# Attention on one Trainium2 core: the last 64 queries of two steps scored in the four quarters of the TensorE array, zero rows under the last keys' values, and an attention order written out as a list

## The chip, the cores and the metric

One core of one Trainium2 chip. The metric is the time of one execution in microseconds of device time; the median of three is given. One further execution was profiled, and all rows below are from it. Engines: PE (TensorE; PEld are its weight loads), DVE (VectorE), ACT (ScalarE), POOL (GpSimd), SP (the queue that issues most DMAs). Each runs its own instructions strictly in the order of the program.

## What is computed

Causal attention in f32 for 2 batches of 12 heads, 448 tokens and head size 64, then two feed-forward layers of 896 tokens, 768 to 2048 to 768.

```python
scores = scale * np.matmul(q, k.transpose(0, 1, 3, 2))      # 2, 12, 448, 448
scores = np.where(mask, -1000000000.0, scores)              # keys after the query
attn = np.exp(scores - np.max(scores, axis=-1, keepdims=True))
attn = attn / (np.sum(attn, axis=-1, keepdims=True) + 1e-09)
x = np.matmul(attn, v)            # then heads side by side: 896 x 768
h = x @ w_in;  x = (h * np.clip(h + 3.0, 0.0, 6.0) / 6.0) @ w_out
h = x @ w2_in; x = (np.maximum(h, 0.0) + alpha * np.minimum(h, 0.0)) @ w2_out
```

## The kernel before

**Attention** goes in 12 steps (`Step`, 2 batches by 6 pairs of heads). The two heads of a pair are two sides: side 0 has rows 0 to 63 of the q and k tiles and side 1 rows 64 to 127, so that the scores of both sides can use two row halves of the array. The 448 queries are three chunks of 128 (chunks 0, 1, 2, with 128, 256 and 384 keys) and a tail of 64 queries with all 448 keys (chunk 3). The tail of both sides stands in one PSUM bank, side 0 on partitions 0 to 63 and side 1 on 64 to 127; with 64 rows and 64 columns each, its two matmuls use two opposite quarters of the array (L123). Per step:

- `scores` (L133 for chunks, L123 for the tail): PE writes q times k into banks of the pool `ps_s` (5 banks).
- `soften`: for each of 7 row groups DVE adds the mask and takes the maximum (L143), then ACT takes the exponential with its sum (L147).
- `normalise`: DVE takes the reciprocals (L151, L152), POOL multiplies the rows by them (L158); for the last step ACT does three of the rows (L156).
- `flip` 0 to 3: PE transposes four 128 by 128 blocks (L173) into a bank of `ps_t` (2 banks), DVE or ACT copies them out (L174). Flip 3 is the tail's.
- `weigh`: PE multiplies with v (L187 for chunks, L194 for the tail) into one bank of `ps_v` (1 bank); the fourth block of tail keys is keys 320 to 447, of which only the upper 64 rows are used (`keys = slice(D, P)`), a quarter of the array for each side.
- `gather`: ACT and DVE split the result into a high and a low part (L75, L76).

Every f32 matmul is two PE instructions. The order is a fixed software pipeline under a manual schedule: step n scores, step n-1 is normalised, step n-2 flipped, step n-3 weighed, step n-4 gathered. From n = 2 on each step also has one bite of `Pieces.convert`, five bites for each of the first three weight pieces, which ACT and DVE turn from 64-bit words into a high and a low part (L230 to L244). After the loop the last steps are flipped and weighed, and the first two units (`unit`, 18 matmuls each, in six bites) of the first layer go in between, in spare banks (tile name s).

**Feed-forward layers**: per unit or output tile three matmuls of 128 by 448 for each 128 rows (L266 to L268, f32r), while ACT and DVE convert the next weight piece and apply the activation. The first matmul whose output is named m begins that stage for good.

SP issues the loads of q, k and v for a step (L93 to L95) up to three steps ahead, and the raw weight pieces (L214).

Of the kernel before, what the change touches and what calls it, by code (L numbers as in the profile page):

```python
# [25 lines left out]
CUTS = ((0, 5), (5, 10), (10, 16))  # L26
ENGINES = {getattr(mybir.EngineType, n) for n in ("PE", "DVE", "Activation", "Pool", "SP")}
AHEAD = 5
MASK = -1.0e9 * D ** 0.5
SCALE = 1.0 / D ** 0.5  # L30


def f32(t):
# [3 lines left out]
class Step:  # L37


    def __init__(self, b, c):  # L40
        self.b, self.c = b, c


@with_exitstack
def fused_kernel(ctx: ExitStack, tc: tile.TileContext, q, k, v, w1i, w1o, w2i, w2o, alpha, out):
# [40 lines left out]

    def load(s):
        s.q = att.tile([P, S], F32, tag="q", name="q", bufs=4)  # L90
        s.k = att.tile([P, S], F32, tag="k", name="k", bufs=4)
        s.v = att.tile([P, 2, NCH + 1, D], F32, tag="v", name="v", bufs=6)
        nc.sync.dma_start(out=s.q, in_=q[s.c, :, s.b])  # L93
        nc.sync.dma_start(out=s.k, in_=k[s.c, :, s.b])
        nc.sync.dma_start(out=s.v, in_=v[s.c, s.b])  # L95

    def half(side):
# [5 lines left out]
    def begin(s):  # L103
        s.e = [att.tile([P, 6 * P], F32, tag="e", name="e", bufs=6) for _ in range(2)]
        s.et = att.tile([P, S], F32, tag="et", name="et")
        s.nm = att.tile([P, 7], F32, tag="nm", name="nm")
        s.sm = att.tile([P, 7], F32, tag="sm", name="sm")
        s.s, s.a = {}, {}

        s.rows = {}  # L110
        for j in range(NCH):
            for side in range(2):
                n = (j + 1) * P
                s.rows[j, side] = (s.e[side][:, OFF[j]:OFF[j] + n], mask[:, TAIL - n:TAIL], 2 * j + side)
        s.rows[NCH, 0] = (s.et, mask_tail, 2 * NCH)

    def scores(s, *chunks):

        if NCH in chunks:
            bank = ps_s.tile([P, BANK], F32, tag="s", name="s")[:, 0:S]  # L120
# [17 lines left out]
    def soften(s, *chunks):  # L138
        for j in chunks:
            for side in range(1 if j == NCH else 2):  # L140
                e, m, i = s.rows[j, side]
                nm, sm = s.nm[:, i:i + 1], s.sm[:, i:i + 1]
                nc.vector.tensor_tensor_reduce(  # L143
                    out=e, in0=s.s[j, side], in1=m, scale=-SCALE, scalar=3.0e38,
                    op0=ALU.add, op1=ALU.min, accum_out=nm,
                )
                nc.scalar.activation(e, e, AF.Exp, bias=nm, scale=-1.0, accum_out=sm)  # L147

    def normalise(s, others=()):
# [3 lines left out]
        for j, side in ((0, 0), (2, 0), (0, 1), (2, 1), (1, 0), (1, 1), (3, 0)):  # L153
            e, m, i = s.rows[j, side]
            if (j, side) in others:
                nc.scalar.activation(e, e, AF.Copy, scale=r[:, i:i + 1])  # L156
            else:
                nc.gpsimd.tensor_scalar(e, e, r[:, i:i + 1], 1.0, ALU.mult, ALU.mult)  # L158

    def flip(s, g, engine):  # L160


        t = ps_t.tile([P, BANK], F32, tag="t", name="t")
        if g < 2:
            todo = [(g, j, 0) for j in range(NCH)] + [(g, 2, 2)]
        elif g == 2:
            todo = [(side, j, 1) for side in range(2) for j in (1, 2)]
# [6 lines left out]
        (nc.scalar.copy if engine else nc.vector.tensor_copy)(a, t)  # L174
        if g < 2:
            s.a[g, 0], s.a[g, 2] = a[:, 0:TAIL], a[:, TAIL:BANK]
        elif g == 2:
            s.a[0, 1], s.a[1, 1] = a[:, 0:2 * P], a[:, 2 * P:4 * P]
        else:
            s.a["tail"] = a  # L180

    def weigh(s, bank=None):

        s.o = ps_v.tile([P, NT], F32, tag="o", name="o") if bank is None else bank
        for kc in range(NCH):
            for side in range(2):
# [12 lines left out]

# [121 lines left out]

    def attention():

        steps = [Step(b, c) for b in range(B) for c in range(KIN)]
        last = len(steps)
        loaded = 0
        runs = []
        ahead = [pieces.convert(i) for i in range(3)]

        def bites(run, count):  # L330
            for _ in range(count):
                next(run)

        for n in range(last):
            while loaded < min(last, n + 3):
                load(steps[loaded])
                loaded += 1
            if n == 1:
                pieces.load_to(1)
                nc.sync.dma_start(out=alpha_sb, in_=alpha)  # L340
            if n == 4:
                pieces.load_to(3)
            now, before, turned, weighed = (steps[n - i] if n >= i else None for i in range(4))
            if n == 0:
                begin(now)
                scores(now, 0, 2)
            scores(now, 1)
            soften(now, 0)
            if before:
                normalise(before)  # L350
            soften(now, 2)
            if turned:
                flip(turned, 0, 0)
                flip(turned, 1, n % 2)
            scores(now, NCH)
            if n >= 4:
                gather(steps[n - 4])
            soften(now, 1)
            if n + 1 < last:
                begin(steps[n + 1])  # L360
                scores(steps[n + 1], 0, 2)
            soften(now, NCH)
            if turned:
                flip(turned, 2, 1)
                flip(turned, 3, 0)
            if weighed:
                weigh(weighed)
            if n >= 2:
                next(ahead[(n - 2) // 5])

        def spare():
            return ps_s.tile([P, BANK], F32, tag="s", name="s")[:, 0:NT]

        runs.append(unit(0, 0, 0, *pieces.parts[0], spare()))
        normalise(steps[last - 1], ((2, 1), (1, 1), (NCH, 0)))
        for g in range(4):
            flip(steps[last - 2], g, g % 2)
        gather(steps[last - 4])
        bites(runs[0], 2)
        weigh(steps[last - 3])  # L380
        gather(steps[last - 3])
        weigh(steps[last - 2], spare())
        gather(steps[last - 2])
        bites(ahead[2], 1)
        for g in range(4):
            flip(steps[last - 1], g, g % 2)
        bites(ahead[2], 1)
        runs.append(unit(0, 0, 1, *pieces.parts[1], spare()))
        bites(runs[0], 3)
        weigh(steps[last - 1])  # L390
        gather(steps[last - 1])
        bites(runs[0], 1)
        bites(ahead[2], 3)
        bites(runs[1], 6)

    with ExitStack() as att_ctx:
        gp["first"] = ctx.enter_context(tc.tile_pool(name="g_first", bufs=1))
# [59 lines left out]
```

## Time and profile before

| | us |
|---|---|
| median of three runs (lowest, highest) | 566.55 (566.23, 566.59) |
| profiled execution | 566.77 |
| its span, first to last instruction | 564.9 |
| PE, DVE, ACT, POOL busy in the span | 551.8, 324.3, 320.3, 41.0 |
| first main-stage matmul (name m) starts at | 100.49 |

Busy time of PE is from modelled ends: two matmuls whose rows overlap count once. The start of one group of PE instructions to the start of the next (its pitch) tells what the group costs when PE never waits.

### The profile page before, as it was taken

How to read it: one execution, taken by the hardware profiler on the slowest of the kernel's cores; microseconds unless marked ns; L12 is line 12 of the kernel's file. 1: busy time of each engine (PE TensorE's matmuls, PEld its weight loads, DVE VectorE, ACT ScalarE, POOL GpSimd, SP SyncE). 2: the span in 40 equal slices, each digit the busy share in tenths (PEclk: the TensorE clock that was granted, in tenths of full speed). 3: DMA queues.
4: the chain of work that ended last, by engine and by line, in shares of the span. 5: the costliest groups of instructions: out<-in, count | busy, mean ns of one | idle time of the engine just before them, and what ended most of it. 6: DMA issues, size and time to landing. Idle time of an engine off the chain costs nothing.

```text
span 564.9 us, 7892 instructions
## 1 busy us (share of the span) xinstructions
PE 551.8 (98%) x3024; PEld 484.3 (86%) x3024; DVE 324.3 (57%) x577; ACT 320.3 (57%) x591; POOL 41.0 (7%) x92
## 2 busy tenths in 40 slices
PE   6999989999999999999999999999999999999997
PEld 3566657989999999999999999999999999999996
DVE  4888862588866576554444547777766634333400
ACT  6977773477665555443444457777777634344210
POOL 3745440000000000000000000000000000000000
PEclk9999999999999999999999999999999999999999
DMA  8363300145422233334333333333232343443000
GB/s 295 139 224 108 131 2 1 56 143 198 163 102 53 98 102 115 128 103 116 106 136 118 113 111 113 112 113 111 94 103 57 106 153 120 125 136 118 17 32 34
DMA packets 16885, 62.25 MB, mean 110 GB/s; under 512 B 2000, under 2 KB 6608, under 8 KB 16848
## 3 DMA queue, kind: packets, MB, share of 16 engines
q1 hardware_dynamic: 15120, 59.00, 31.8%
q10 hardware_dynamic: 1728, 2.75, 1.3%
q8 instruction: 24, 0.39, 0.3%
q14 instruction: 13, 0.11, 0.1%
HBM read 58.99 MB, written 2.75 MB: 109 GB/s over the span
## 4 chain that ended last, share of the span: by engine, by line
PE 85%; ACT 8%; DVE 4%; issue 2%; DMA 0%; SPq 0%; ACTq 0%; DVEq 0%
PE m L268 27%; PE m L266 27%; PE m L267 27%; ACT e L147 4%; PE t L173 1%; DVE e L143 1%; DVE a L174 1%; PE s L133 1%; ACT et L147 1%; PE o L187 1%; ACT xh L75 1%; ACT a L174 1%; DVE wf L238 0%; DMA k<-k_t 0%; DVE raw L235 0%
## 5 line engine op out<-in xcount | busy, mean ns | idle before, releaser
L266 PE MATMUL m<-gh,hi 128*128 128x448 f32 x384 | 140.2, 365 | 0.0
L268 PE MATMUL m<-gh,lo 128*128 128x448 f32 x384 | 140.2, 365 | 0.0
L267 PE MATMUL m<-gl,hi 128*128 128x448 f32 x384 | 140.2, 365 | 0.0
L268 PE MATMUL m<-xh,lo 128*128 128x448 f32 x372 | 135.7, 366 | 0.3 <-DVE lo L244 0.3
L267 PE MATMUL m<-xl,hi 128*128 128x448 f32 x372 | 136.0, 365 | 0.0
L266 PE MATMUL m<-xh,hi 128*128 128x448 f32 x372 | 135.9, 365 | 0.0
L244 DVE TENSOR_TENSOR lo<-wf,hi 128x768 fp32r<-128x768 f32 (+1 forms) x68 | 61.8, 911 | 88.0 <-ACT hi L242 86.1
L242 ACT CAST hi<-wf 128x768 fp32r<-128x768 f32 (+1 forms) x68 | 54.0, 796 | 83.9 <-PE m L267 80.1
L235 DVE SCALAR_TENSOR_TENSOR raw<-wf,raw 128x768 uint32<-128x768 uint32 (+1 forms) x68 | 61.9, 912 | 60.9 <-ACT wf L230 58.8
L233 ACT ACTIVATE raw<-raw 128x768 uint32<-128x768 uint32 (+1 forms) x68 | 59.3, 872 | 41.4 <-DMA raw<-w1o 17.2
L268 PEld LDWEIGHTS m<-gh,lo 128*128 128x128 f32 x384 | 72.1, 188 | 5.7
L267 PEld LDWEIGHTS m<-gl,hi 128*128 128x128 f32 x384 | 72.1, 188 | 5.7
L266 PEld LDWEIGHTS m<-gh,hi 128*128 128x128 f32 x384 | 72.1, 188 | 5.7
L268 PEld LDWEIGHTS m<-xh,lo 128*128 128x128 f32 x372 | 69.9, 188 | 6.3 <-DVE lo L244 0.7
L266 PEld LDWEIGHTS m<-xh,hi 128*128 128x128 f32 x372 | 69.9, 188 | 5.7
L267 PEld LDWEIGHTS m<-xl,hi 128*128 128x128 f32 x372 | 69.9, 188 | 5.7
L230 ACT ACTIVATE wf<-raw 128x768 f32<-128x768 f32 (+1 forms) x68 | 57.9, 851 | 22.1 <-DVE lo L244 22.1
L238 DVE SCALAR_TENSOR_TENSOR wf<-wf,raw 128x768 uint32<-128x768 uint32 (+1 forms) x68 | 61.8, 909 | 1.5
L75 ACT CAST gh<-hg 128x448 fp32r<-128x448 f32 x64 | 36.0, 562 | 36.9 <-DVE hg L276 20.5
L76 DVE TENSOR_TENSOR gl<-hg,gh 128x448 fp32r<-128x448 f32 x64 | 39.9, 623 | 23.9 <-ACT gh L75 23.6
L147 ACT ACTIVATE e<-e,nm 128x128 f32<-128x128 f32 (+2 forms) x72 | 35.8, 500 | 17.7 <-DVE nm L143 17.3
L158 POOL TENSOR_SCALAR e<-e,r 128x128 f32<-128x128 f32 (+1 forms) x70 | 32.0, 482 | 40.8 <-DVE r L152 14.8
(60 smaller groups left out, 406.4 us busy)
## 6 DMA issues: line engine op xcount, KB each, us to landing
raw<-w1i SPq DMA_DIRECT2D x16, 768.0 KB, 4.4
raw<-w2i SPq DMA_DIRECT2D x16, 768.0 KB, 4.4
raw<-w1o SPq DMA_DIRECT2D x12, 640.0 KB, 4.0
raw<-w2o SPq DMA_DIRECT2D x12, 640.0 KB, 4.1
raw<-w1o SPq DMA_DIRECT2D x6, 768.0 KB, 4.4
raw<-w2o SPq DMA_DIRECT2D x6, 768.0 KB, 4.4
v<-v_t SPq DMA_DIRECT2D x12, 256.0 KB, 3.6
q<-q_t SPq DMA_DIRECT2D x12, 224.0 KB, 4.3
```

The lines of the kernel that those rows point to most:

```text
L75: nc.scalar.copy(hi, src)
L76: nc.vector.tensor_sub(lo, src, f32(hi))
L147: nc.scalar.activation(e, e, AF.Exp, bias=nm, scale=-1.0, accum_out=sm)
L230: fixed(nc.scalar.activation(f32(w), f32(high), AF.Copy, scale=2.0 ** -112))
L233: fixed(nc.scalar.activation(low, low, AF.Copy, bias=-0.4999, scale=2.0 ** -29 * (1 - 2.0 ** -16)))
L235: fixed(nc.vector.scalar_tensor_tensor(out=low, in0=w, scalar=3, in1=low, op0=ALU.logical_shift_left, op1=ALU.bitwise_or))
L238: fixed(nc.vector.scalar_tensor_tensor(out=w, in0=w, scalar=0x80000000, in1=low, op0=ALU.bitwise_and, op1=ALU.bitwise_or))
L242: nc.scalar.copy(hi[:, 0:width], f32(w))
L244: nc.vector.tensor_sub(lo[:, 0:width], f32(w), f32(hi[:, 0:width]))
L266: nc.tensor.matmul(ps, lhsT=hi[:, w], rhs=xh, start=start, stop=False)
L267: nc.tensor.matmul(ps, lhsT=hi[:, w], rhs=xl, start=False, stop=False)
L268: nc.tensor.matmul(ps, lhsT=lo[:, w], rhs=xh, start=False, stop=stop)
```

## The change

`scores_tail` takes two steps: four matmuls of the tails, one for each quarter of the array. The second step of each pair is `odd`: its sides change places on the partitions of its bank (`at`). v gets 64 zero rows between key 384 and the last 64 keys, so that `weigh` uses all 128 rows for the fourth block too; the part of the last flip's output that belongs to the zero rows is there already. `attention` no longer has a loop over steps: it walks through the words of `PLAN`. The first letter is the function (s scores, t scores_tail of a pair, e soften, n normalise, f flip, w weigh, g gather, c a bite of convert, u a bite of a unit), two digits are the step (or the piece or unit), and the rest are its arguments: chunks; chunk and side; which of the seven rows ACT normalises; number and copying engine of the flip. Six matmuls on a zero tile stand in front. q and k have buffers for four steps, v for six; k of step 0 is issued from ACT's queue instead of SP's, v one step after q and k. The copies of the four flips have two buffers each, where all shared eight.

```diff
+QK_AHEAD, V_AHEAD = 4, 6
+WARM = 6
...
+PLAN = """
+s001 s0002 e0011 e0010 e0001 e0000 e0021 t00 s011 e0020 e0030 e0130 s0102 e0110 e0111 e0100 n00 e0101
+s021 e0121 s0202 e0120 e0211 e0210 e0200 e0221 e0201 e0220 t02 n0104 f000v f002v s0302 e0230 f003v f001v
+e0330 s031 e0311 e0300 n02 e0321 e0301 e0320 f011v f013v e0310 w00 t04 e0430 f010v f012v g00 s041 c00
+s0402 f023a e0421 e0420 n03 e0530 f021v e0401 e0411 e0410 w01 f020v f022v s051 g01 s0502 e0510 e0400
+e0521 e0511 f032v e0501 f031a e0520 w02 s061 n04 e0500 e0611 f033v g02 f030a s0602 t06 c01 e0610 n051
+e0621 f040v e0630 f042v e0600 e0620 e0601 w03 f041v f043v g03 s071 c01 s0702 e0720 f051a e0730 e0711 n06
+f053v w04 t08 e0710 e0701 e0700 e0721 e0830 f052v f050v n07 s081 g04 c00 s0802 e0810 e0811 e0801 f063v
+e0930 f060v w05 g05 f070a f062a s0902 e0800 e0820 e0821 f072v f061a e0901 s091 e0920 n080 e0900 e0910
+e0911 f071v f073a w06 e0921 s101 c01 g06 c01 s1002 f083a e1000 f081a n09 e1020 w07 e1011 e1021 e1001 t10
+f080a c01 e1010 e1030 f082v g07 s111 f091a f090a s1102 n102 f092a e1130 c00 f093a w08 c00 e1111 e1120
+e1121 e1110 f100v f101v e1101 w09s e1100 f103a c00 f102a n11234 u00 u01 c02 u01 f111v f112a g09 u01 g08
+c02 f110a f113v w10s w11 u00 u01 c02 u01 g11 u00 u00 g10 u00 c02 u00 c02 u01
+"""
...
-    def __init__(self, b, c):
-        self.b, self.c = b, c
+    def __init__(self, b, c, odd):
+        self.b, self.c, self.odd = b, c, odd
+        self.s, self.rows = {}, None
+
+    def at(self, side):
+        return side ^ self.odd
...
-        nc.sync.dma_start(out=s.k, in_=k[s.c, :, s.b])
+        queue.dma_start(out=s.k, in_=k[s.c, :, s.b])
+
+    def load_v(s):
+        s.v = att.tile([P, 2, NCH + 1, D], F32, tag="v", name="v", bufs=V_AHEAD)
...
-        if NCH in chunks:
-            bank = ps_s.tile([P, BANK], F32, tag="s", name="s")[:, 0:S]
-            for side in range(2):
-                d = half(side)
-                nc.tensor.matmul(bank[d], lhsT=s.q[d, TAIL:S], rhs=s.k[d, 0:S], start=True, stop=True)
-            s.s[NCH, 0] = bank
-            return
...
+    def scores_tail(*pair):
+
+        for s in pair:
+            s.s[NCH, 0] = ps_s.tile([P, BANK], F32, tag="s", name="s")[:, 0:S]
+        for s in pair:
+            for side in range(2):
+                d = half(side)
+                nc.tensor.matmul(
+                    s.s[NCH, 0][half(s.at(side))], lhsT=s.q[d, TAIL:S], rhs=s.k[d, 0:S], start=True, stop=True
+                )
...
-        a = att.tile([P, BANK], F32, tag="a", name="a", bufs=8)
+        a = att.tile([P, BANK], F32, tag=f"a{g}", name="a", bufs=2)
...
-            keys = slice(D, P) if kc == NCH else slice(0, P)
             for side in range(2):
                 nc.tensor.matmul(
-                    s.o[half(side), TAIL:S], lhsT=s.v[keys, side, kc],
-                    rhs=s.a["tail"][keys, kc * P + side * D:kc * P + (side + 1) * D],
+                    s.o[half(side), TAIL:S], lhsT=s.v[:, side, kc],
+                    rhs=s.a["tail"][:, kc * P:(kc + 1) * P][:, half(s.at(side))],
                     start=(kc == 0), stop=(kc == NCH),
                 )
...
+        warm = att.tile([P, P], F32, tag="warm", name="warm", bufs=1)
+        nc.vector.memset(warm, 0.0)
+        bank = ps_t.tile([P, BANK], F32, tag="t", name="t")
+        for _ in range(WARM):
+            nc.tensor.matmul(bank[:, 0:P], lhsT=warm, rhs=warm, start=True, stop=True)
+
+        for word in PLAN.split():
+
+            while qk < len(steps) and (qk < QK_AHEAD or scored[qk - QK_AHEAD] == 3):
+                load_qk(steps[qk], nc.sync if qk else nc.scalar)
+                qk += 1
+                while vs < min(len(steps), V_AHEAD + weighed, qk - 1):
+                    load_v(steps[vs])
+                    vs += 1
+                if qk == QK_AHEAD:
+                    pieces.load_to(1)
+                    nc.sync.dma_start(out=alpha_sb, in_=alpha)
+                elif qk == QK_AHEAD + 2:
+                    pieces.load_to(3)
...
+            what, n, rest = word[0], int(word[1:3]), word[3:]
+            s = steps[n]
+            if what == "s":
+                scores(s, *map(int, rest))
...
+            elif what == "t":
+                scores_tail(s, steps[n + 1])
...
+            elif what == "w":
+                weigh(s, spare() if rest else None)
...
-    vt = np.stack([vt[:, :, :, i:i + P] for i in (0, P, 2 * P, S - P)]).transpose(2, 1, 4, 3, 0, 5)
+    vt = np.insert(vt, [TAIL] * D, 0, axis=3).reshape(B, KIN, 2, NCH + 1, P, D).transpose(1, 0, 4, 2, 3, 5)
```

## Rows read from the trace of the kernel before

**Rows 1.** Busy time by stage: window, its length, then busy us (instructions) of PE, PEld, DVE, ACT, POOL, granted clock, DMA share and GB/s. The four windows are the start of attention, its steady steps, its end, and the feed-forward stage.

```profile
4.08:20.44 16.36, 14.71 (x84) 8.28 (x84) 12.41 (x60) 12.84 (x47) 7.73 (x17) 1.00 0.86 303
20.44:74.56 54.12, 54.11 (x481) 33.48 (x480) 44.23 (x161) 43.06 (x138) 27.13 (x57) 1.00 0.38 131
74.56:100.49 25.93, 22.48 (x193) 16.75 (x193) 11.28 (x24) 12.94 (x30) 3.95 (x9) 1.00 0.00 1
100.49:564.90 464.41, 460.50 (x2269) 425.70 (x2267) 256.35 (x335) 250.19 (x378) 0.00 (x0) 1.00 0.33 107
```

**Rows 2.** PE's timeline over one steady step: start us, us, line, operation, count. The last row is the same place in the next step.

```profile
27.15 0.97 PE L123 MATMUL s<-k,q 64*64 64x448 f32 x4
28.05 1.14 PE L133 MATMUL s<-k,q 64*128 64x128 f32 x8
29.12 0.66 PE L173 MATMUL t<-ident,e 128*128 128x128 f32 x4
29.61 0.60 PE L173 MATMUL t<-ident,et 128*128 128x128 f32 x4
30.14 1.52 PE L187 MATMUL o<-a,v 128*64 128x384 f32 x12
31.48 0.78 PE L194 MATMUL o<-a,v 128*64 128x64 f32 x16
32.19 0.70 PE L133 MATMUL s<-k,q 64*128 64x256 f32 x4
32.83 1.09 PE L173 MATMUL t<-ident,e 128*128 128x128 f32 x8
33.85 0.97 PE L123 MATMUL s<-k,q 64*64 64x448 f32 x4
```

**Rows 3.** PE's timeline, feed-forward matmuls: the first of the main stage and one 55 matmuls later.

```profile
100.49 0.37 PE L266 MATMUL m<-xh,hi 128*128 128x448 f32 x1
...
111.86 0.37 PE L267 MATMUL m<-xl,hi 128*128 128x448 f32 x1
```

**Rows 4.** PE's timeline in a window of 0.1 us around 20.5: the tail's instructions that run in it.

```profile
20.44 0.59 PE L123 MATMUL s<-k,q 64*64 64x448 f32 x2
```

**Rows 5.** PE's timeline in windows of 0.05 us: the end of one weigh, from its last two instructions on 128 rows (with the two behind them), from the first of the four on 64 rows, and the scores that follow.

```profile
25.07 0.43 PE L194 MATMUL o<-a,v 128*64 128x64 f32 x4
25.23 0.33 PE L194 MATMUL o<-a,v 64*64 64x64 f32 x4
25.49 0.49 PE L133 MATMUL s<-k,q 64*128 64x256 f32 x2
```

**Rows 6.** Timeline of all engines, the first 14 us (rows of the first step's way to its first flip).

```profile
0.73 1.28 ACT L147 ACT_TABLE_LOAD   x1 [0.73 <-PEq L447]
...
0.74 0.38 SPq L93 DMA_DIRECT2D q<-q_t  x1
...
1.17 0.42 SPq L94 DMA_DIRECT2D k<-k_t  x1
...
4.08 2.93 PE L133 MATMUL s<-k,q 64*128 64x128 f32 x12 [4.08 <-DMA k<-k_t]
...
6.28 0.29 DVE L143 CUSTOM_DVE_ANT_0 e<-s,mask 128x128 f32<-128x128 f32 x1 [6.28 <-PE s L133]
...
6.94 1.35 PE L123 MATMUL s<-k,q 64*64 64x448 f32 x4
...
10.95 2.75 POOL L158 TENSOR_SCALAR e<-e,r 128x128 f32<-128x128 f32 x6 [8.06 <-DVE r L152]
...
13.22 1.09 PE L173 MATMUL t<-ident,e 128*128 128x128 f32 x8
```

**Rows 7.** Busy time of L133 alone, in the first two microseconds of the first scores and in a steady step: the same eight instructions (chunks 0 and 2; where 10 stand, two are of the next group).

```profile
4.08:6.18 2.10, 2.10 (x10) 1.55 (x12) 1.00 0.88 206
28.05:29.12 1.07, 1.07 (x8) 0.52 (x8) 1.00 1.00 413
```

**Rows 8.** The page: clock granted to PE, in tenths of full speed over 40 equal slices, and the two copies of L174 that take the flips out (count, busy us, mean ns, idle us before them).

```profile
PEclk9999999999999999999999999999999999999999
...
L174 DVE COPY a<-t 128x512 f32<-128x512 f32 x29 | 19.4, 685 | 5.0 <-PE t L173 4.9
L174 ACT COPY a<-t 128x512 f32<-128x512 f32 x19 | 10.8, 567 | 1.9 <-PE t L173 1.9
```

**Rows 9.** Groups of instructions by line from 0 to 120 us: the rows that ACT normalises (count, busy us, mean ns, idle us before).

```profile
L156 ACT ACTIVATE e<-e,r 128x384 f32<-128x384 f32 (+1 forms) x2 | 1.0, 554 | 0.5 <-DVE r L152 0.5
```

**Rows 10.** Busy time by step, in the columns of rows 1: the first and the last of eight steps from one tail to the next.

```profile
20.44:27.15 6.71, 6.71 (x62) 4.15 (x61) 4.32 (x19) 6.71 (x23) 4.37 (x10) 1.00 0.04 13
...
67.44:74.56 7.12, 7.12 (x61) 4.43 (x60) 6.83 (x29) 6.07 (x20) 4.52 (x10) 1.00 0.32 112
```

**Rows 11.** What PE waited for from 8 to 110 us: us in total, times, longest.

```profile
PE t L173 <- ACT a L174: 2.4, 3, 1.1
PE t L173 <- DVE a L174: 1.2, 2, 0.9
PE o L187 <- DVE xl L76: 0.9, 2, 0.6
```

**Rows 12.** Timeline of SP and ACT: the load of the fourth raw weight piece, and the next L230 on ACT after those of the first three pieces.

```profile
59.63 0.37 SPq L214 DMA_DIRECT2D raw<-w1i  x1
...
109.89 0.91 ACT L230 ACTIVATE wf<-raw 128x768 f32<-128x768 f32 x1
```

More of the change, by code (lines that the diff above doesn't have):

```diff
@@ L84, in split_x, with load_qk @@
         xs[blk, c] = (xh, xl)
[L89 to L92, printed above, removed]
+    def load_qk(s, queue):
+        s.q = att.tile([P, S], F32, tag="q", name="q", bufs=QK_AHEAD)
+        s.k = att.tile([P, S], F32, tag="k", name="k", bufs=QK_AHEAD)
         nc.sync.dma_start(out=s.q, in_=q[s.c, :, s.b])
-        nc.sync.dma_start(out=s.k, in_=k[s.c, :, s.b])
+        queue.dma_start(out=s.k, in_=k[s.c, :, s.b])
+    def load_v(s):
+        s.v = att.tile([P, 2, NCH + 1, D], F32, tag="v", name="v", bufs=V_AHEAD)
         nc.sync.dma_start(out=s.v, in_=v[s.c, s.b])
@@ L107, in begin @@
         s.sm = att.tile([P, 7], F32, tag="sm", name="sm")
-        s.s, s.a = {}, {}
+        s.a = {}
         s.rows = {}
@@ L136, in scores, with soften, normalise @@
             at += n
[L138 to L145, printed above, removed]
-                )
-                nc.scalar.activation(e, e, AF.Exp, bias=nm, scale=-1.0, accum_out=sm)
-    def normalise(s, others=()):
+    def scores_tail(*pair):
[6 more added lines that the diff above has]
+                    s.s[NCH, 0][half(s.at(side))], lhsT=s.q[d, TAIL:S], rhs=s.k[d, 0:S], start=True, stop=True
+                )
+    def soften(s, j, side):
+        if s.rows is None:
+            begin(s)
+        e, m, i = s.rows[j, side]
+        nm, sm = s.nm[:, i:i + 1], s.sm[:, i:i + 1]
+        nc.vector.tensor_tensor_reduce(
+            out=e, in0=s.s[j, side], in1=m, scale=-SCALE, scalar=3.0e38,
+            op0=ALU.add, op1=ALU.min, accum_out=nm,
+        )
+        nc.scalar.activation(e, e, AF.Exp, bias=nm, scale=-1.0, accum_out=sm)
+    def normalise(s, others):
         r = att.tile([P, 7], F32, tag="r", name="r")
@@ L152, in normalise @@
         nc.vector.reciprocal(r, r)
-        for j, side in ((0, 0), (2, 0), (0, 1), (2, 1), (1, 0), (1, 1), (3, 0)):
-            e, m, i = s.rows[j, side]
-            if (j, side) in others:
+        for n, row in enumerate(((0, 0), (2, 0), (0, 1), (2, 1), (1, 0), (1, 1), (NCH, 0))):
+            e, m, i = s.rows[row]
+            if n in others:
                 nc.scalar.activation(e, e, AF.Copy, scale=r[:, i:i + 1])
@@ L173, in flip @@
             nc.tensor.transpose(t[:, i * P:(i + 1) * P], e, ident)
-        (nc.scalar.copy if engine else nc.vector.tensor_copy)(a, t)
+        (nc.scalar.copy if engine == "a" else nc.vector.tensor_copy)(a, t)
         if g < 2:
@@ L322, in attention @@
     def attention():
[L324 to L327, printed above, removed]
+        steps = [Step(b, c, c % 2) for b in range(B) for c in range(KIN)]
         ahead = [pieces.convert(i) for i in range(3)]
[L330 to L394, printed above, removed]
+        units = {}
+        scored, weighed, qk, vs = [0] * len(steps), 0, 0, 0
+        warm = att.tile([P, P], F32, tag="warm", name="warm", bufs=1)
+        nc.vector.memset(warm, 0.0)
@@ new lines, in attention @@
+        bank = ps_t.tile([P, BANK], F32, tag="t", name="t")
[13 more added lines that the diff above has]
+                    pieces.load_to(3)
+            while vs < min(len(steps), V_AHEAD + weighed, qk):
+                load_v(steps[vs])
+                vs += 1
+            what, n, rest = word[0], int(word[1:3]), word[3:]
+            s = steps[n]
+            if what == "s":
+                scores(s, *map(int, rest))
+                scored[n] += 1
+            elif what == "t":
+                scores_tail(s, steps[n + 1])
+                scored[n] += 1
+                scored[n + 1] += 1
+            elif what == "e":
+                soften(s, int(rest[0]), int(rest[1]))
+            elif what == "n":
+                normalise(s, tuple(map(int, rest)))
+            elif what == "f":
+                flip(s, int(rest[0]), rest[1])
+            elif what == "w":
+                weigh(s, spare() if rest else None)
+                weighed += 1
+            elif what == "g":
+                gather(s)
+            elif what == "c":
+                next(ahead[n])
+            elif what == "u":
+                if n not in units:
+                    units[n] = unit(0, 0, n, *pieces.parts[n], spare())
+                next(units[n])
@@ L396, in fused_kernel, with spare @@
+    def spare():
+        return ps_s.tile([P, BANK], F32, tag="s", name="s")[:, 0:NT]
     with ExitStack() as att_ctx:
```

## The prediction, made before the changed kernel ran

> **What bounds the kernel now.** I read the page first, then busy time by stage, PE's timeline over one step, the timeline of the start and the waits of PE. By stage [rows 1]: PE is busy 54.11 of 54.12 us in the steady steps, 460.50 of 464.41 in the feed-forward stage, but 14.71 of 16.36 at the start of attention and 22.48 of 25.93 at its end. DVE is busy 82% (44.23 of 54.12) and ACT 80% (43.06) in the steady steps and far less elsewhere. So the feed-forward stage is PE's from 100.49 us to the end, and a change of attention is worth what it moves the first main-stage matmul.
>
> PE's busy time hides overlap, so I count by pitch. A steady step [rows 2]: tail 0.90, chunks 0 and 2 1.07, flips 2 and 3 0.49 + 0.53, weigh 1.34 + 0.71, chunk 1 0.64, flips 0 and 1 1.02; together 6.70 (27.15 to 33.85), without a wait. The 36 matmuls of the two units that lie in attention cost 0.207 each ((111.86 - 100.49) / 55 [rows 3]), 7.44 in all. PE's work up to 100.49 is 12 x 6.70 + 7.44 = 87.84; the other 12.65 us are losses. I split them at the bounds of the stages [rows 1], with the pitches of the steady step [rows 2]:
> - **a**, before the first matmul: 4.08.
> - **b**, 4.08 to 20.44: 16.36 less the work done in it, which by the loop is four chunk pairs 0 and 2 (4.28), four chunks 1 (2.56), three tails (2.70) and six flips (3.06), 12.60: 3.76.
> - **c**, 20.44 to 74.56: 54.12 less 8 x 6.70: 0.52.
> - **d**, 74.56 to 100.49: 25.93 less the remaining 21.64: 4.29.
>
> **The change, part by part.**
>
> *Tails in four quarters.* Now a tail is four instructions of 448 columns in a pitch of 0.90; two of them run at the same time, both in flight from 20.44 on [rows 4], so each two cost 0.45. The change issues eight for two steps. If four run at once a pair of steps costs little over 0.90; if still only two, 4 x 0.45 = 1.80, as now. Between 0.90 and 1.80 I take 0.95: the rows that use column halves at once (weigh's two sides) and row halves at once (chunks' two sides) both show overlap, chunks 0 and 2 having 2 x (128 + 384) columns in 1.07 where the tail's 896 need 0.90 [rows 2], and the four quarters are the product of the two. The extra 0.05 is for four more instructions (16 small ones of weigh's tail cost 0.71, 0.044 each, partly hidden). Gain: 12 x 0.90 - 6 x 0.95 = 5.10.
>
> Two instructions at once in one PSUM bank is also where a rule of the Trainium skill can be held against the trace. Today's two quarters lie on different rows, write the same bank and start together [rows 4]. The Trainium skill's page TensorEngine Tiling (Array Packing), section Gotcha 1: PSUM Pressure, says that different row tiles can't reach the same PSUM bank at the same time. By that rule each bank's two matmuls would take turns, the best would be two at a time, and this part would gain nothing; the trace disagrees, since it shows two in one bank.
>
> *Zero rows under v.* The four instructions of the last block run on 64 rows; the first of them start 0.16 after the last two on 128 rows [rows 5], where two instructions at weigh's mean pitch take 0.09. The 0.07 over is what I give to the change of shape, 12 x 0.07 = 0.84; bounds 0 and 12 x 0.16 = 1.9. The multiplications by zero add no instructions; v's transfer keeps its size.
>
> PE's work thus falls by 5.94.
>
> *The start (a).* k of step 0 goes from the second place in SP's queue to ACT's. It was issued at 1.17 and used at 4.08, 2.91 later [rows 6]. Issued at 0.74 it is there at 3.65; issued after the 1.28 us table load that now begins at 0.73, it is there at 4.92. The table load belongs to the first exponential, which stands behind the load in the program, so I take the early side. The six zero matmuls lie on PE ahead of the scores: at the slow pace of the first scores (2.10 for 512 columns on each side [rows 7]) 128 columns cost 0.52, six 3.2; begun after a memset at about 1.0, they end near 4.2, so they can hold the scores by half a microsecond. I take 3.9 for a: -0.18.
>
> *The first rounds (b).* The first eight score instructions took 2.10 against 1.07 later [rows 7], and the first tails 1.35 against 0.97 [rows 6, 2], although the page shows the granted clock at full speed (2.4 GHz) throughout [rows 8]; before them PE was idle. DVE's first operation waited for all eight (6.28), and everything after it in the first rounds is the chain DVE, ACT, POOL up to the first flip at 13.22 [rows 6]. The plan scores chunk 1 first, four instructions, 0.64 at full or 1.26 at half pace, so DVE begins at about 4.6 to 5.2, 1.1 to 1.7 earlier; I take 1.4, and 0.4 for the tail at full pace. The first flip stands after 20 softens in the plan, yet needs only the normalised rows of step 0, so it comes earlier by the same amount. b = 3.76 - 1.8 = about 2.0: -1.76. Bounds 0.6 (no loss but the chain's own) and 3.76.
>
> *The steady order (c).* DVE and ACT keep their work: the plan has 29 flips copied by DVE and 19 by ACT, as now [rows 8], and the same softens, gathers and bites. Only eight rows are normalised on ACT instead of three, 5 x 0.55 = 2.8 at most [rows 9], of over 90 us. But PE's eight steps shrink from 53.6 to 49.6, so DVE rises from 82% to about 88%. The first of the eight steps has DVE busy 4.32 of 6.71 and ACT 6.71; the last has DVE 6.83 of 7.12 and is 0.42 longer than the rest [rows 10]: when DVE is near full, PE waits. Between 0.52 as now and 8 x 0.42 = 3.4 I take 1.5: +0.98. The fixed lists make this sensitive: a late e on DVE holds every flip copy and xl behind it, and by them PE's next transposes and weigh.
>
> *The end (d).* PE's waits are for copies a and for xl [rows 11]: the last two steps' flips stand next to each other, with two banks and nothing else to do. The plan puts w08, w09 and half-microsecond bites of units between them, and between g and the next w. I leave one wait of the size seen (0.9) and 0.8 for refilling: 1.7, -2.59; bounds 0.8 and 4.29.
>
> *What lies under cover.* Raw pieces 1 and 2 are queued on SP right behind k of step 5, 1.5 MB or 5 us at the 303 GB/s of the start [rows 1]; behind them wait v of step 5 and q of step 6, first used after w02, over 10 us later. Without that cover each would be up to 5 us late. v is issued one step after q and k, and is first read by w00, word 48 of the plan. Raw piece 3 waits for the third bite of piece 0, now just before w08, near 70 us instead of the issue at 59.63; ACT first reads it at 109.89 [rows 12], about 100 after the change, so some 25 us are spare. The feed-forward stage needs piece 2 one unit pair (36 matmuls, 7.4 us) after its start, and the plan ends its bites before that start. I count 0.
>
> **The sum.** -5.94 - 0.18 - 1.76 + 0.98 - 2.59 = -9.49. The profiled execution took 566.77 for a span of 564.9, so 1.87 lie outside; 555.41 + 1.87 = 557.28. It lay 0.22 above the median, so the median forecast is 557.1.
>
> **Rivals.**
> - *The written order brings nothing*: b, c and d stay as they are, because losses on PE reappear as waits for DVE and ACT at 88%. For it: the 7.12 step. Against: the waits at the end have an empty DVE and ACT (11.28 and 12.94 of 25.93 [rows 1]). Only the work and a count: -6.12, 560.4. With c at its bound of 3.4, 563.3.
> - *Only two quarters at a time*: the change then doesn't do what its name says. The tails keep 1.80 a pair, +5.10, 562.2. The bank rule of the Trainium skill named above would be one such cause. Against: both kinds of overlap are seen [rows 2].
> - *Slower: quarters take turns one by one.* Eight instructions at 0.45 cost 3.60 a pair, 2.65 over the forecast, +15.9: 573.0. Decisive from 0.95 + 9.49 / 6 = 2.53 a pair on. For it: nothing here shows two instructions sharing rows and two sharing columns at once. Against: today's two opposite quarters overlap [rows 4].
>
> **How the numbers follow.** Forecast 0.70, order brings nothing 0.20, two at a time 0.06, one by one 0.04. Predicted time 557.1. The forecast's own bounds: quarters at 0.90, full 1.9 for zero rows, a 3.65, b 0.6, c 0.52 and d 0.8 would be 5 lower, and not all at once; I take 553.2 as the low end. The upper end, 562.2, takes in the order that brings nothing and reaches the two at a time. A measurement of this kernel can tell about 0.2% (1.1 us) from no change. Only one by one is slower: 0.04; within 0.2% only where an order worse than bounded eats both gains: 0.02; faster 0.94.
>
> **What will show it.** The first main-stage matmul near 91 instead of 100.49. The pitch of a double tail near 0.95 in PE's timeline; 1.8 or more proves the second or third rival. Weigh's tail below 0.71. DVE's first operation before 5.3. Waits of PE in the end below 2 us, and some new waits for DVE or ACT in the middle. The feed-forward stage as long as before, 464.4. The prediction is wrong if the main stage starts after 96, or if it grows by a wait for converted pieces.

## The result and the profile after

| | before | after |
|---|---|---|
| median, us | 566.57 | 552.96 |
| ratio (95% interval) | | 0.9763 (0.9746 to 0.978) |
| span of the profiled execution | 564.9 | 550.9 |
| first main-stage matmul (name m) | 100.49 | 86.78 |
| feed-forward stage from there | 464.41 | 464.12 |

The kernel is 13.6 us faster. The forecast was 557.1 with a range from 553.2 to 562.2: the sign was right, the gain was too small by 4.1 us, and the time lies 0.24 below the range. Most of the 4.1 comes from one step of the prediction, the waits that it expected in the middle and at the end of attention (terms c and d). All of the gain but 0.3 us is attention's: the main stage begins 13.71 earlier. A few executions, of the kernel before too, are some 9 us longer; all medians here and below leave them out.

PE's timeline after the change (start, us, line, operation, count), first the first rounds, then a steady stretch, the two waits and the first main-stage matmul. These rows answer to the steady step [rows 2] and to the weigh's end [rows 5]; the last one is the same as [rows 3].

```profile
6.24 0.98 PE L168 MATMUL s<-k,q 64*64 64x448 f32 x8
7.15 2.99 PE L156 MATMUL s<-k,q 64*128 64x256 f32 x18
10.83 1.13 PE L156 MATMUL s<-k,q 64*128 64x128 f32 x6 [0.69 <-DVE nm L177]
11.89 0.98 PE L168 MATMUL s<-k,q 64*64 64x448 f32 x8
12.81 1.09 PE L207 MATMUL t<-ident,e 128*128 128x128 f32 x8
...
18.93 0.64 PE L227 MATMUL o<-a,v 128*64 128x64 f32 x16
19.50 0.98 PE L168 MATMUL s<-k,q 64*64 64x448 f32 x8
20.41 1.09 PE L207 MATMUL t<-ident,e 128*128 128x128 f32 x8
21.43 1.57 PE L156 MATMUL s<-k,q 64*128 64x256 f32 x12
22.93 0.66 PE L207 MATMUL t<-ident,et 128*128 128x128 f32 x4
...
23.96 1.52 PE L221 MATMUL o<-a,v 128*64 128x384 f32 x12
...
58.86 0.66 PE L207 MATMUL t<-ident,et 128*128 128x128 f32 x4 [0.89 <-POOL et L192]
...
70.11 1.00 PE L207 MATMUL t<-ident,e 128*128 128x128 f32 x7 [0.39 <-POOL e L192]
...
86.78 0.36 PE L299 MATMUL m<-xh,hi 128*128 128x448 f32 x1
```

A double tail costs 0.91 (19.50 to 20.41), where two tails cost 1.80. Weigh's tail costs 0.57 (18.93 to 19.50) instead of 0.71. Chunk 1 with chunks 0 and 2 right behind it costs 1.50 (21.43 to 22.93), where they cost 0.64 + 1.07 apart. And from 20 us to the main stage PE waits only twice for longer than 0.2, both times for POOL.

PE's timeline after, in a window of 0.04 us behind 19.52, answers to [rows 4]: four instructions in flight from 19.50 on.

```profile
19.50 0.61 PE L168 MATMUL s<-k,q 64*64 64x448 f32 x4
```

The start after, all engines [rows 6]: k of step 0 issued by ACT (its table load stands behind it, at 1.17), the zero matmuls, the first scores and DVE's first operation.

```profile
0.74 0.40 ACTq L121 DMA_DIRECT2D k<-k_t  x1
...
1.05 2.93 PE L367 MATMUL t<-warm 128*128 128x128 f32 x12 [1.05 <-DVE warm L364]
...
4.13 2.18 PE L156 MATMUL s<-k,q 64*128 64x256 f32 x12
...
5.52 0.42 DVE L177 CUSTOM_DVE_ANT_0 e<-s,mask 128x256 f32<-128x256 f32 x1 [4.52 <-PE s L156]
```

Busy time by stage after, in the columns of [rows 1]: start, middle, end, feed-forward stage.

```profile
4.13:19.50 15.37, 14.63 (x117) 9.30 (x117) 13.80 (x65) 13.51 (x51) 6.95 (x15) 1.00 1.02 391
19.50:69.39 49.89, 49.01 (x493) 33.14 (x489) 44.73 (x153) 45.32 (x140) 29.75 (x55) 1.00 0.33 104
69.39:86.78 17.39, 17.00 (x156) 14.14 (x153) 9.59 (x25) 11.65 (x28) 3.73 (x8) 1.00 0.27 91
86.78:550.90 464.12, 460.23 (x2269) 425.54 (x2267) 256.75 (x336) 249.73 (x379) 0.00 (x0) 1.00 0.32 105
```

DVE and ACT are busy 90% and 91% of the middle, more than the 88% of the prediction, and PE idles 0.9 of 49.9.

**The prediction's sum with measured terms.** Work after: 12 x (6.70 - 0.90 - 0.14) + 6 x 0.91, and 36 unit matmuls at 0.203: 80.70. The loss is the rest of 86.78, 6.08, split as before: 4.13 before the first scores; from there to 19.50, 15.37 less 13.65 of work; the middle to 69.39, 49.89 less 49.94; the end, 17.39 less 17.11. The work is counted with the old order's pitches for all groups but the tails, so a group that the new order makes cheaper shows as a smaller loss; that is why the middle comes out at -0.05.

| term | forecast | measured |
|---|---|---|
| tails in four quarters | -5.10 | -5.34 |
| zero rows | -0.84 | -1.68 |
| a, before the first scores | -0.18 | +0.05 |
| b, first rounds | -1.76 | -2.04 |
| c, middle | +0.98 | -0.57 |
| d, end | -2.59 | -4.01 |
| unit matmuls 0.203 instead of 0.207 | | -0.12 |
| sum | -9.49 | -13.71 |
| feed-forward stage | 0 | -0.29 |

### The profile page after: what moved, and what is told of

Its sections match the earlier page's. It is cut to its first block, busy times and chain, and to the rows that moved or that the text cites. A ratio compares the mean times of both kernels' runs of the same rounds, so it can differ in the third digit from the quotient of the medians.

```text
span 550.9 us, 7924 instructions
## 1 busy us (share of the span) xinstructions
PE 543.8 (99%) x3036; PEld 484.8 (88%) x3036; DVE 325.0 (59%) x578; ACT 321.5 (58%) x596; POOL 42.6 (8%) x87
## 4 chain that ended last, share of the span: by engine, by line
PE 94%; DVE 2%; POOL 1%; DMA 1%; ACT 1%; issue 1%; POOLq 0%; ACTq 0%
PE m L301 27%; PE m L299 27%; PE m L300 27%; PE t L207 4%; PE s L156 3%; PE o L221 2%; POOL e L192 1%; PE s L168 1%; PE o L227 1%; DVE e L177 1%; DMA k<-k_t 1%; PE s L221 1%; PE s L299 0%; PE s L301 0%; PE s L300 0%
## 5 line engine op out<-in xcount | busy, mean ns | idle before, releaser
L192 POOL TENSOR_SCALAR e<-e,r 128x128 f32<-128x128 f32 (+2 forms) x64 | 32.4, 526 | 32.5 <-DVE nm L177 15.2
```

## The experiments

Before was run beside all of them (medians 566.5 to 566.8). Differences below are of medians, against the 552.96 of the changed kernel unless another is named. The theory: PE sets the time of the new order, so each PE term counts in full, and the order removed most waits. The main rival: DVE and ACT, 90% busy, set it.

### Quarters, alone undone

```diff
-        steps = [Step(b, c, c % 2) for b in range(B) for c in range(KIN)]
+        steps = [Step(b, c, 0) for b in range(B) for c in range(KIN)]
```

> The changed kernel, but both steps of a pair of tails use the same two opposite quarters (no step is odd); order, zero rows and start stay. Theory (four quarters at once is worth its pitch): a double tail takes 4 x 0.45 = 1.80 instead of 0.91 on PE, 6 x 0.89 = 5.3 us more, 558.3. Rival (DVE and ACT, 90% busy in the middle of the changed kernel, pace it): part of the 5.3 lies in time in which PE would have waited, 2 us more or less, near 555.

Measured 556.51: 3.6 more; the profiled spans differ by 4.1 (555.0), the main stage begins at 90.98, 4.2 later. PE's timeline of this run, the second and the third double tail and the main stage:

```profile
12.38 1.72 PE L168 MATMUL s<-k,q 64*64 64x448 f32 x8
14.04 1.09 PE L207 MATMUL t<-ident,e 128*128 128x128 f32 x8
...
20.73 1.72 PE L168 MATMUL s<-k,q 64*64 64x448 f32 x8
...
90.98 0.36 PE L299 MATMUL m<-xh,hi 128*128 128x448 f32 x1
```

Two tails that take turns in the same quarters cost 1.66, not 1.80: two tails next to each other cost 0.14 less than two apart. Undoing the quarters thus adds 6 x 0.75 = 4.5 to PE's work, and most of it (3.6 to 4.2) reaches the end. The expected 5.3 took 1.80 for the pair. From the third double tail to the main stage it takes 70.25, after the change 67.28: the four double tails there (4 x 0.75 = 3.0) count in full, so PE does set the time of middle and end, and the rival's 2 us is out.

### Zero rows, alone undone

```diff
         for kc in range(NCH + 1):
+            keys = slice(D, P) if kc == NCH else slice(0, P)
...
-                    s.o[half(side), TAIL:S], lhsT=s.v[:, side, kc],
-                    rhs=s.a["tail"][:, kc * P:(kc + 1) * P][:, half(s.at(side))],
+                    s.o[half(side), TAIL:S], lhsT=s.v[keys, side, kc],
+                    rhs=s.a["tail"][keys, kc * P:(kc + 1) * P][:, half(s.at(side))],
```

> The changed kernel, but the fourth block of weigh's tail uses only the upper 64 rows again (the zero rows are loaded and not used). Theory (the change of shape costs PE, as the pitch of weigh's tail shows, 0.57 against 0.71): 12 x 0.14 = 1.7 us more, 554.6. Rival (the pitch difference comes from what stands behind it): no difference.

Measured 554.09 (three runs, 553.8 to 555.1), 1.1 more, two thirds of what was expected. PE's timeline of this run, one weigh's tail and the double tail behind it:

```profile
43.79 0.72 PE L228 MATMUL o<-a,v 128*64 128x64 f32 x14
...
45.26 1.09 PE L207 MATMUL t<-ident,e 128*128 128x128 f32 x8
```

Nine of the twelve weigh's tails cost 0.70 to 0.72 here, as in the kernel before. The other three stand in front of a double tail, which has the shape of the four matmuls on 64 rows, and these cost nothing more: weigh's tail and double tail take 1.46 to 1.47 together (43.79 to 45.26), with the zero rows 1.48. So 9 x 0.14 = 1.3 is what PE's work grows by, and the rival, that it depends on what stands behind, is partly right. In the other nine, half the multiplications of this block cost more time than all of them.

### The start

Without the zero matmuls (`WARM = 0`):

> The changed kernel without the six zero matmuls at the start. Theory (they let PE reach the full pace earlier, and the first operations of DVE wait for the scores): chunks 1, 0 and 2 of step 0 run at half pace throughout, 1.5 us longer, and the first tails too; 1 to 1.5 us more, 554.2. Rival (the chain over DVE, ACT and POOL sets the first flip anyway): below 0.3 more.

Measured 554.0, 1.05 more: the theory. Its first scores and tails, PE's timeline:

```profile
4.39 2.93 PE L156 MATMUL s<-k,q 64*128 64x256 f32 x12 [4.39 <-DMA k<-k_t]
7.25 1.77 PE L168 MATMUL s<-k,q 64*64 64x448 f32 x8
```

The first twelve score instructions take 2.86 (4.39 to 7.25), with the zero matmuls 1.50 to 2.58 in the profiled executions that begin with the same two words, 2.11 in that of the changed kernel. The first double tail takes 1.77; with the zero matmuls it was at full pace (0.98) in that of the changed kernel and at half pace in that of the next run. The zero matmuls began at 1.05 and ended at 3.98, before the first scores at 4.13, so they held nothing up there.

k of step 0 on SP's queue again (`load_qk(steps[qk], nc.sync)`):

> The changed kernel with k of step 0 on SP's queue again, second behind q. Theory (the first scores wait for it): issued 0.43 later, it lands up to 0.4 later, 553.3. Rival (q and k share the transfer, whoever issues them): no difference.

Measured 553.05: no difference, the rival. The first scores begin at 3.96, not later than with k on ACT's queue (4.13); who issues k doesn't matter, and a did not shrink. That q and k share the transfer is the rival's reason; this run doesn't show it. The first double tail of this run:

```profile
6.17 1.91 PE L168 MATMUL s<-k,q 64*64 64x448 f32 x8
```

It is at half pace, 0.93 longer than in the changed kernel, and the main stage begins only 0.12 later (86.90), or 0.29 later counted from the first scores. Most of the first tail's pace is thus hidden by the wait for DVE that follows it.

Chunk 1 of step 0 second instead of first:

```diff
-s001 s0002 e0011 e0010 e0001 e0000 e0021 t00
+s0002 s001 e0011 e0010 e0001 e0000 e0021 t00
```

> The changed kernel with the first two words of the list exchanged: chunks 0 and 2 of step 0 are scored first, chunk 1, which DVE reads first, second. Theory (DVE's first operation sets the first rounds, which are DVE's and ACT's): DVE begins 0.8 to 1 later, and so does the main stage, 553.9. Rival (the first rounds wait for data or for PE): below 0.3.

Measured 553.83, 0.87 more. DVE's first operation begins at 6.99 instead of 5.52, 0.25 of it because the first scores began later in this execution. The first rounds are bound by when DVE can start, as term b had it.

### The order: neighbours on PE

Five times a flip is put between chunk 1 and chunks 0 and 2 of a step. Two of the five edits:

```diff
-s041 c00 s0402 f023a
+s041 c00 f023a s0402
...
-s101 c01 g06 c01 s1002 f083a
+s101 c01 g06 c01 f083a s1002
```

> The changed kernel with one flip put between chunk 1 and chunks 0 and 2 of steps 4, 5, 7, 8 and 10, which stand next to each other in the list. Theory (PE pays about 0.2 for each change of the kind of matmul: together they cost 1.50, apart 1.07 + 0.64): 5 x 0.21 = 1.05 more, 554.0. Rival (the 0.2 is hidden or an effect of how the ends are modelled): no difference.

Measured 557.11, 4.2 more, far beyond the 1.05. PE's timeline of this run, around the first split and around the last, and PE's granted clock (the column before the DMA share) there:

```profile
22.07 0.70 PE L145 MATMUL s<-k,q 64*128 64x256 f32 x4
22.88 0.63 PE L196 MATMUL t<-ident,et 128*128 128x128 f32 x4
23.44 1.14 PE L145 MATMUL s<-k,q 64*128 64x128 f32 x8
...
25.10 1.52 PE L210 MATMUL o<-a,v 128*64 128x384 f32 x12
...
61.06 1.07 PE L196 MATMUL t<-ident,et 128*128 128x128 f32 x4 [1.74 <-POOL et L181]
62.06 2.08 PE L145 MATMUL s<-k,q 64*128 64x128 f32 x8
```

```profile
58.00:61.00 3.00, 1.32 (x25) 0.85 (x20) 2.96 (x5) 2.62 (x9) 3.00 (x4) 1.00 0.00 0
61.00:63.00 2.00, 1.94 (x10) 1.61 (x12) 0.03 (x1) 0.95 (x2) 0.00 (x1) 0.53 0.72 209
63.00:65.00 2.00, 2.00 (x10) 0.76 (x8) 0.79 (x5) 0.49 (x2) 0.02 (x1) 0.61 0.44 184
```

The direction of the theory holds: the first split costs 25.10 - 22.07 = 3.03 up to the weigh, where the same four groups cost 23.96 - 21.43 = 2.53 after the change; it also parts two flips, as do the next three splits, at 0.36 each. More came on top. The last split moved a flip ahead of the scores that had covered POOL, so the wait of 0.89 became 1.74; behind it the granted clock fell to 0.53, close to the lower of the two levels (1.2 GHz), and eight scores took 2.08 instead of 1.14. That slow stretch is not in every execution: three of six, the profiled one among them, have a mean granted clock of 0.997 over the whole span and take 557.9 to 558.0, the other three have 1.00 and take 555.7 to 556.4. So the size doesn't measure the neighbours alone: five splits of 0.36 to 0.50 each are some 2 us, the longer wait 0.85, and the slow stretch 1.7 where it occurs.

The two waits for POOL, taken away:

```diff
-n080
+n0806
...
-n102
+n1024
```

> The changed kernel with one more row of step 8 (the tail's) and one of step 10 (chunk 1, side 0) normalised on ACT instead of POOL. PE's two longest waits after the start are for these rows on POOL (0.89 and 0.39). Theory (POOL's chain of seven rows ends last there): both vanish, 1.2 less, 551.7. Rival (ACT, 91% busy in that stretch, has no room): no change or up to 1 us more.

Measured 551.43, ratio to before 0.9735 (0.9722 to 0.9749), 1.5 less than the changed kernel: the theory, and the fastest version of this study. From the third double tail to the main stage it takes 66.05 instead of 67.28, the 1.2 that was expected. ACT, busy 91% in the middle, had room for both rows. PE's waits of this run over the whole span hold none for POOL:

```profile
PE t L367 <- DVE warm L364: 1.1, 1, 1.1
PE s L156 <- DVE nm L177: 0.8, 1, 0.8
PE m L301 <- DVE lo L277: 0.3, 1, 0.3
PE s L156 <- DMA k<-k_t: 0.3, 1, 0.3
```

### The old order with the other parts

The list now repeats the loop and the end of the kernel before. With the double tail at each even step, and the same with both steps in the same quarters:

```diff
+PLAN = """
+...
+s041 e0400 e0401 n03 e0420 e0421 f020v f021v t04 g00 e0410 e0411 s0502 e0430 f022a f023v w01 c00
+s051 e0500 e0501 n04 e0520 e0521 f030v f031a g01 e0510 e0511 s0602 e0530 f032a f033v w02 c00
+...
+"""
```

> The changed kernel with the old order: the list is written so that it repeats the loop and the end of the kernel before, word by word, only that the tails of two steps stand at the even step. Quarters, zero rows, zero matmuls and loads as in the changed kernel. Theory (the order took away the waits of the end and the separation of the scores, but not a pacing by DVE or ACT): the end loses about 4 us again and the joined scores 1.5, 558 to 559, with no waits in the middle. Rival (as in the prediction: with PE's step 0.5 shorter DVE and ACT at 88% hold PE in the middle, whatever the order): waits of 1 to 3 us in the middle too, 560 to 561.

> Old order and the tails of a pair in the same two quarters; zero rows, zero matmuls and loads as in the changed kernel. If quarters and order add up, 5.3 more than the run with the old order and four quarters, about 563.5; against the kernel before only zero rows (1.7) and the start (1 to 2) are left. If quarters pay less in the old order, because DVE and ACT hold PE there, the distance is below 4.

Measured 574.12 and 570.78: both slower than the kernel before, and the one with four quarters by more. Neither theory nor rival had this. Of the run with four quarters, PE's longest wait in total (us in all, times, longest), and one of its places in the timeline with the granted clock behind it:

```profile
PE s L157 <- DVE nm L178: 7.6, 7, 1.8
```

```profile
56.54 0.98 PE L169 MATMUL s<-k,q 64*64 64x448 f32 x8
57.45 0.48 PE L157 MATMUL s<-k,q 64*128 64x128 f32 x2
59.78 1.13 PE L157 MATMUL s<-k,q 64*128 64x128 f32 x6 [1.84 <-DVE nm L178]
...
62.60 2.41 PE L222 MATMUL o<-a,v 128*64 128x384 f32 x12
```

```profile
55.00:60.00 5.00, 3.16 (x25) 1.76 (x27) 3.80 (x16) 3.97 (x13) 3.36 (x7) 1.00 0.17 52
60.00:62.60 2.60, 2.60 (x15) 1.73 (x13) 0.62 (x4) 2.20 (x8) 0.00 (x0) 0.70 0.01 3
62.60:65.40 2.80, 2.80 (x29) 1.65 (x28) 2.30 (x11) 2.37 (x8) 1.07 (x3) 0.67 0.00 0
```

Two tails hold two of the five banks, the second one for a whole step longer than it was held before. Chunk 1 has two more, so the next scores get the fifth bank and must wait for DVE to read another. PE waits 7.6 in all, and behind three of its four waits of 1.37 to 1.84 the clock falls (weigh's first part takes 2.41 instead of 1.52); behind the one of 1.75, which ends at 45.11, it stays at 1.00. With the same two quarters these waits are 6.1 in all, none above 1.46, and the clock falls behind none of them in its profile. This is most of why four quarters lose here. Their gain is there (0.91 a pair, 4.5 in all), but 1 less the granted clock, times the length of the three slow stretches (11.4 to 18.0, 60.0 to 65.4 and 76.6 to 82.0), adds up to an estimated 5.1, and the waits are 1.5 longer: 2.1 of the 3.3 by this count. All four executions have a mean clock of 0.991 to 0.994, with the same two quarters 0.997 to 1.00. Without the new order the double tail thus makes the kernel slower.

So the order had to be tried with single tails, as in the kernel before (a word t at every step, and every step in the same two quarters); zero rows, zero matmuls and loads stay:

```diff
-                scores_tail(s, steps[n + 1])
-                scored[n] += 1
-                scored[n + 1] += 1
+                scores_tail(s)
+                scored[n] += 1
```

> The changed kernel with the old order written as a list and each step's tail alone at its old place (two quarters). Zero rows, zero matmuls and the loads stay as in the changed kernel, so that against it only the order and the quarters are undone. Theory (the parts add up: 1.6 for the zero rows and 1.2 for the zero matmuls, as their own runs gave): 566.6 - 2.8 = 563.8, and the order is worth 563.8 - 556.5 = 7.3 without the quarters. Rival (the loads in their new sequence also matter): 562 or less.

Measured 565.65, ratio to before 0.9978 (0.9968 to 0.9987): 1.0 better than before, not 2.8 (zero rows and zero matmuls gave 1.1 and 1.05 by themselves, 2.2 together). Its timeline of PE in the two steps ahead of the end:

```profile
66.99 0.97 PE L169 MATMUL s<-k,q 64*64 64x448 f32 x4
68.28 1.61 PE L157 MATMUL s<-k,q 64*128 64x128 f32 x8 [0.33 <-DVE nm L178]
...
74.41 0.97 PE L169 MATMUL s<-k,q 64*64 64x448 f32 x4
```

PE's step is 6.56 in most places, 0.14 shorter by the zero rows, but this one takes 7.42 (74.41 - 66.99), where before it took 7.12 [rows 10]. From the tail of step 3 to that of step 11 eight steps take 53.86 (20.55 to 74.41), where they took 54.12: of 8 x 0.14 = 1.1 saved only 0.26 is left. The rest became short waits for DVE. The start gained nothing either: the tail of step 3 begins at 20.55, where it began at 20.44. In the old order PE, busy 100% of the middle by the page's count, was on the edge of not being the bound, which is what the prediction feared of the new one. Against the run with the new order and the same two quarters (556.51), the order, with the tails in pairs, is worth 9.1.

The end's order alone, on top of that run:

```diff
-n11356 f100v f101a f102v f103a g08 u00 u00 w09 g09 w10s g10 c02 f110v f111a f112v f113a c02
-u00 u00 u00 w11 g11 u00 c02 c02 c02 u01 u01 u01 u01 u01 u01
+n11356 f100v f101a g08 u00 u00 f102v f103a u00 u00 w09 g09 f110v f111a c02 u00 u01 w10s g10
+f112v f113a c02 u01 u01 u01 w11 g11 u00 c02 c02 c02 u01 u01
```

> As the run with the old order and single tails, but in the end, after the loop, the bites of the two units stand between the flips of the last two steps and the weighs, and nothing else is changed. Theory (the end loses 4.3 because flips and weighs stand next to each other with nothing in between): 2 to 2.5 less than that run, 561.5. Rival (the end is the chain of the last steps' softmax, whatever PE does meanwhile): less than 0.5.

Measured 566.06, no gain on 565.65. The main stage does begin 2.6 earlier (97.23 against 99.81), as the theory said, but then PE waits in it:

```profile
102.96 0.47 PE L300 MATMUL m<-xh,hi 128*128 128x448 f32 x1 [1.84 <-DVE hg L310]
```

The wait is for the activation of the second unit on DVE. In both lists the last bite of the first unit stands behind w11, and the three last bites of piece 2 stand in front of the second unit's activation, on DVE and ACT; that activation begins at 102.29 on DVE in this run and at 102.47 without the change. So the chain of DVE and ACT behind the last weigh did not move, and PE only reaches it sooner. The end's time is gained only if these bites are moved too; the changed kernel's list, which spreads them, has no such wait.

The neighbours alone, on top of the run with single tails: `s{n+1}02 s{n+1}1` stand together at the end of each round.

> As the run with the old order and single tails, but chunk 1 of each step is scored right behind chunks 0 and 2, not at the start of the next round. Theory (a change of the kind of matmul costs PE 0.2): 11 x 0.2 = 2.2 less than that run, 561.6. Rival (five banks are then all held, and PE waits for DVE): no gain, or slower by as much as the run with two tails at a time in the old order.

Measured 571.87, 6.2 slower than without: the rival. PE's waits:

```profile
PE s L157 <- DVE nm L178: 5.6, 6, 1.6
```

By the list all five banks are held again. The joined pair that saves 0.2 in the new order costs a bank wait in the old one.

## Why the prediction was right and where it was wrong

- **Tails in four quarters**: right. 0.95 was forecast, 0.91 measured, four in flight at once, and undoing them costs 3.6. Both rivals on the quarters fall: two at a time would have shown 1.66 to 1.80, one by one 3.6. The bank rule, TensorEngine Tiling (Array Packing), section Gotcha 1: PSUM Pressure, of the Trainium skill isn't borne out here: four matmuls run at once, and each of the two banks is written by two row halves.
- **Zero rows**: right kind, half the size. 0.07 was taken for the change of shape, it is 0.14 a step (0.57 against 0.71) where the next group has another shape, and nothing in front of a tail, so that undoing them costs 1.1. Only the start of the shape was priced, not what the next kind of matmul pays behind it.
- **Start (a, b)**: a did not shrink, since k's transfer isn't faster from ACT's queue. The size of b was right (2.04 for 1.76), by luck, since its parts were not those of the prediction. DVE's first operation came 0.76 earlier (5.52 against 6.28) where 1.4 was taken, and missed the forecast "before 5.3"; the first flip came 0.41 earlier (12.81 against 13.22) where 1.8 was taken. The first scores, at a better pace, gave 0.75 (2.11 against 2.86), the first tail 0.37, most of which the run with k on SP's queue shows to be hidden in the new order, and the scores of steps 1 and 2 lost 0.6 more than before in waiting for DVE. The largest part, 1.6, is in step 3 of the old order: its scores of chunks 0 and 2 took 1.50 instead of 1.07, and then PE waited for a copy that ACT made. The new order has neither, and the prediction had no term for them. PE's timeline before:

```profile
19.45 1.06 PE L173 MATMUL t<-ident,e 128*128 128x128 f32 x8 [1.09 <-ACT a L174]
```

- **Middle and end (c, d)**: the wrong step. The prediction put 1.5 for waits at 88% load in the middle and left 1.7 at the end, 3.2 together; measured are -0.05 and 0.28, 0.23 together, both below the least that it allowed (0.52 and 0.8). That is about 1.28 for two waits, both of POOL's rows and none of DVE or ACT, less 5 x 0.21 = 1.05 for joined scores, a gain that the prediction had no term for: it took PE's pitches as the same in any order. That POOL could hold PE was not in it either. The 1.5 came from the long step of the old order [rows 10], and the old order does show it (the loss of its middle is 53.86 - 8 x 6.56 = 1.4 with a step 0.14 shorter). It doesn't carry over to another order: the new one runs DVE and ACT at 90% with no such wait. The end's waits were expected to shrink to one; there is only the 0.39.
- **The rival that the order brings nothing** is the most wrong of all: the order, with the tails in pairs, is 9.1 of the difference, two thirds, when it is changed ahead of the quarters. And the parts don't add up: the quarters are worth 3.6 in the new order and cost 3.3 in the old one (574.12 against 570.78), there by longer waits and the clock behind them.

What stays open: why the new order can run DVE and ACT at 90% without a wait. That it keeps a bank free and something between a flip and its use fits all runs, but no run isolates it, and moving single parts of it into the old order gave nothing.

## What to carry to other kernels

Price a reorder by itself: PE's pitch of a group depends on its neighbours (0.14 to 0.2 us a change of kind here), and the load of the other engines says little of what an order will wait for. A saving on an engine that shows 100% busy can still vanish (1.1 became 0.26), so look at a step that is longer than the rest before trusting the share. When a change holds a buffer longer, count the buffers at every word of the order: one bank too few, with the clock that fell behind the waits, turned a gain of 3.6 us into a loss of 3.3.

## What the runs showed of the hardware

- Changing the shape of f32 matmuls costs PE: chunk scores 1.50 together and 1.71 apart, weigh's tail 0.57 in one shape and 0.71 in two. In front of a double tail, whose matmuls have 64 rows and 64 columns as well, the 0.14 is gone (1.46 to 1.47 for both groups against 1.48).
- Eight f32 instructions in four quarters take 0.91, in two quarters 1.66: four at once, although each bank is written from both row halves.
- A PE wait can cost more than its length. Behind waits of 1.74 and 1.84 us the granted clock was 0.53 and 0.70 in the next 2 to 3 us, and the matmuls there took up to twice as long; in the lowest stretches (13.4 to 16.0 in the old order with four quarters, for one) it was 0.50, the lower level of 1.2 GHz. It isn't a fixed rule: of the waits from 1.37 to 1.84 in the old-order runs and the run with split scores five were followed by such a fall (1.37, 1.46, 1.63, 1.74, 1.84) and four were not (1.37, 1.46, 1.75, 1.84), and by the mean clock the split-scores kernel had the fall in three of six executions, the old order with the new end in five of ten. Behind the waits of 1.16 and below that came after the first scores it stayed at 1.00. The Trainium skill, TensorE: Matmul & The Clock Gate, section Part 1: The HAM clock gate, tells of a clock that falls to half when the engine is idle; these falls agree with it in size, and no run here shows why the other waits had none.
- At the start the matmuls ran at half pace (2.10 for 1.07 [rows 7]) while the profile shows a granted clock of 1.00, also in the run without zero matmuls (2.86 for 1.50): the pace there has to be read from the matmuls, not from that column.
